# Scoring two neighbouring chunks back to back, so that the tensor array changes shape less often

## Chip, cores, metric

One core of a Trainium2 chip. The metric is the device time of one execution in microseconds (us), as the median of the runs; the profile's span (first to last instruction) is some 1.75 us shorter than the time of the same run.

## The reference

A retention layer followed by a mixer, for 4 batches of 768 positions, 8 heads of 64:

```python
state = gamma * state + k_t v_t^T          # per head, t = 0..767
y_t   = q_t @ state / sqrt(64)
u  = x + (x^T @ U @ V)^T                   # x: y of all heads, 768 x 512; rank 32
out = u + relu(u @ w_ch1) @ w_ch2          # 512 -> 2048 -> 512
```

The kernel computes the retention in six chunks of 128 positions a batch: a chunk's scores (k against q, masked causally), times v, plus q times the state that the chunks before have left.

## The kernel before

The attention of batch b runs inside the MLP of batch b-1. The MLP is a list of pieces with costs; each attention step is tied to a fraction of the total cost and goes out at the first piece boundary past it. The parts that matter, cut ("..."):

```python
RINGS = {"mlp": [0, 1, 2], "s": [3, 4], "o": [5], "qk": [6], "st": [7],
         "A": [6, 0], "B": [1], "C": [2]}      # PSUM banks by use; "mlp": [6, 0, 1, 2] for batches 2, 3
def score(b, ci):
    kT, qT = live["k", b, ci // 2][:, ci % 2], q_cols(b, ci)
    sp = [bank("s") for _ in range(2)]
    for h in range(H):                         # 8 matmuls on 64 rows of the array
        r = ds(D * (h % 2), D)
        nc.tensor.matmul(sp[h % 2][:, ts(h // 2, P)], kT[r, h // 2], qT[r, h // 2], ...)
    for i in range(2):                         # 2 masks on VectorE, 128x512 each
        a = rmid.tile([P, 4, P], bf16, tag=f"a{i}", bufs=2, ...)
        nc.vector.tensor_tensor(a, four(sp[i]), causal(mask), op=ALU.mult)
def mix(b, ci):                                # 4 matmuls of q with the state (not for chunk 0),
    o_p = bank("o")                            # 8 of the masked scores with v
    ...
    evac("A", xs[b][:, ci], o_p)               # ScalarE copies the bank out
...
# MLP 1 and 2: 32 "up" pieces (relu on ScalarE, each 4th on VectorE), sums of gT on VectorE
# after pieces 12-15, 16-19, 24-27, two after 31 and one after each of the first two of the 21
# products on the banks A, B and C that follow:
def p1(i): product("A", i, a11, w11, True);  keep("A", i, "a", i, 0)   # keep: VectorE reads A
def p2(i): product("B", i, a12, w21, True);  give("B", i, i, 0, held["a", i])
def p6(i): product("A", i, s2, t2, False);   keep("A", i, "b", i, 1)   # adds to what p1 left in A
order = [(p1, 0), (p1, 1), (p2, 0), (p6, 0), (p6, 1), ...]
...
for f, d in ((state, lag[0]), (score, lag[1]), (mix, lag[2] + more)):
    tracks.append(([part(f, b, i)], at[i] + d, at[i] + d))             # chunk by chunk
```

## Time and profile before

| | before |
|---|---|
| time, runs of the first comparison | 222.66, 223.40, 223.43, 223.38 us |
| span of the profile | 220.9 us |
| PE from the first MLP-up matmul to the last matmul (starts) | 189.52 us |
| switches between array shapes in that stretch | 58, together 5.46 us |
| PE waits over 60 ns in it | 2.47 us in 10 places |

TensorE (PE) carries the kernel. A matmul of N columns normally takes N/2.4 + 2.5 ns to the next start (the medians of the profile of before are 29, 56, 109 and 216 ns for 64, 128, 256 and 512 columns). What lies above that is a switch, where the number of active rows or columns changes, or a wait. Short waits never show as idle time, since a matmul's tail covers some 0.16 us (a 512-column matmul is shown with 0.38 us and the next starts after 0.216).

### The profile page before, as it was taken

The page shows a single profiled execution, that of the slowest core. Times are in us where ns is not written, and L with a number is a line of the kernel's source. Part 1 is how long each engine was busy: PE and PEld are TensorE (multiplying, and loading weights), DVE is VectorE, ACT ScalarE, POOL GpSimd, SP SyncE. Part 2 cuts the span into 40 slices and gives each one's busy share as a digit, 9 for nine tenths or more (in the row PEclk, how much of TensorE's full clock was granted, in tenths as well). Part 3 has the DMA queues.
Part 4 walks back from the last instruction along what each step waited for, and adds up shares of the span by engine and source line. Part 5 has one row for each costly group of instructions (what it writes and reads, how often), then busy time and mean ns, then how long its engine had stood idle before and what let it go on. Part 6 is the DMA issues. An engine that isn't in the chain of part 4 may idle for free.

```text
span 220.9 us, 5520 instructions
## 1 busy us (share of the span) xinstructions
PE 213.1 (96%) x2235; PEld 147.5 (67%) x2235; DVE 146.6 (66%) x306; ACT 91.1 (41%) x187; POOL 83.0 (38%) x121
## 2 busy tenths in 40 slices
PE   6879999999999999999999999999999999999994
PEld 2568754596555554656778884756788856668884
DVE  7578666235775469698896856498868542867443
ACT  3347654475655314775712005767420035551000
POOL 5457869796978767000099900000000000000000
PEclk9999999999999999999999999999999999999999
DMA  6999899999999989999999587900001951000043
GB/s 169 301 293 298 279 356 246 326 380 223 230 235 239 244 195 236 178 324 254 214 238 202 140 186 188 129 0 3 1 3 48 155 205 23 4 0 0 11 158 119
DMA packets 84489, 38.82 MB, mean 176 GB/s; under 512 B 58384, under 2 KB 77552, under 8 KB 84464
## 3 DMA queue, kind: packets, MB, share of 16 engines
q1 hardware_dynamic: 83456, 36.84, 70.7%
q10 hardware_dynamic: 1008, 1.64, 2.2%
q8 instruction: 17, 0.28, 0.6%
q14 instruction: 8, 0.07, 0.1%
HBM read 27.46 MB, written 6.29 MB: 153 GB/s over the span
## 4 chain that ended last, share of the span: by engine, by line
PE 85%; DVE 8%; DMA 2%; ACT 2%; issue 1%; SPq 1%; DVEq 0%; ACTq 0%
PE mlp L755 35%; PE A L647 13%; PE mlp L803 8%; PE C L647 6%; PE B L647 3%; DVE a L512 3%; DMA in<-in_q_dram 2%; PE s L506 2%; DVE gS L600 2%; PE o L528 2%; ACT qT L85 2%; PE st L490 1%; PE mlp L193 1%; PE qk L465 1%; PE o L523 1%
## 5 line engine op out<-in xcount | busy, mean ns | idle before, releaser
L755 PE MATMUL mlp<-uT,w1b 128*128 128x512 f16 (+1 forms) x512 | 88.7, 326 | 0.2 <-DVE gT L760 0.2
L762 ACT ACTIVATE gT<-mlp 128x512 f16<-128x512 f32 (+1 forms) x94 | 45.3, 490 | 59.3 <-PE mlp L755 57.1
L755 PEld LDWEIGHTS <-w1b 128*128 128x128 f16 x512 | 48.3, 98 | 31.1 <-issue 0.3
L760 DVE TENSOR_SCALAR gT<-mlp 128x512 f16<-128x512 f32 (+1 forms) x34 | 18.9, 555 | 27.1 <-PE mlp L755 26.7
L647 PEld LDWEIGHTS <-gT 128*128 128x128 f16 x288 | 27.6, 98 | 3.5
L512 DVE TENSOR_TENSOR a<-s,mask 128x512 bf16<-128x512 f32 x36 | 23.1, 682 | 7.8 <-PE s L506 7.7
L803 PE MATMUL mlp<-w2b,gT 128*128 128x512 f16 x96 | 24.4, 380 | 0.0
L85 ACT ACTIVATE x<-o 128x512 f16<-128x512 f32 x20 | 11.9, 596 | 23.6 <-PE o L528 23.5
L306 POOL TENSOR_TENSOR kd<-in,gk 128x512 bf16<-128x512 f32 x18 | 19.2, 1074 | 5.1 <-DMA in<-in_k_dram 4.2
L647 PEld LDWEIGHTS <-gS 128*128 128x128 f16 x200 | 19.2, 98 | 2.6
L306 POOL TENSOR_TENSOR qd<-in,gq 128x512 bf16<-128x512 f32 x18 | 19.5, 1099 | 1.3 <-DMA in<-in_q_dram 1.2
L647 PE MATMUL A<-w2t,gT 128*128 128x256 f16 x144 | 18.2, 273 | 0.0
L85 ACT ACTIVATE state<-st 64x256 bf16<-64x256 f32 x40 | 15.0, 375 | 5.4 <-PE st L386 3.2
L803 PEld LDWEIGHTS <-gT 128*128 128x128 f16 x96 | 8.1, 98 | 6.9
L304 POOL CAST vd<-in 128x512 bf16<-128x512 f32 x18 | 11.5, 649 | 1.1 <-DMA in<-in_v_dram 0.9
L346 POOL CAST w2b<-in 128x512 f16<-128x512 f32 x16 | 9.6, 613 | 2.0 <-DMA in<-in_moe_w_ch_dram 1.3
L340 POOL CAST w1b<-in 128x512 f16<-128x512 f32 x16 | 9.4, 613 | 2.3 <-DMA in<-in_moe_w_ch_dram 1.9
L647 PE MATMUL B<-w2b,gT 128*128 128x256 f16 x72 | 9.3, 273 | 0.0
L647 PE MATMUL A<-w2t,gS 128*128 128x256 f16 x72 | 9.2, 273 | 0.0
L647 PE MATMUL A<-w2b,gT 128*128 128x256 f16 x72 | 9.0, 273 | 0.0
L565 DVE TENSOR_TENSOR x<-s,x 128x256 f16<-128x256 f32 (+1 forms) x16 | 8.1, 548 | 1.2 <-issue 0.7
L600 POOL COPY gate<-gT 128x1 f16<-128x1 f16 x1 | 0.2, 190 | 22.5 <-DVE gT L760 22.5
(147 smaller groups left out, 283.4 us busy)
## 6 DMA issues: line engine op xcount, KB each, us to landing
in<-in_moe_w_ch_dram SPq DMA_DIRECT2D x32, 256.0 KB, 5.6
in<-in_k_dram SPq DMA_DIRECT2D x24, 256.0 KB, 5.4
in<-in_q_dram SPq DMA_DIRECT2D x24, 256.0 KB, 4.7
in<-in_v_dram SPq DMA_DIRECT2D x24, 256.0 KB, 5.4
out_dram<-o SPq DMA_DIRECT2D x16, 256.0 KB, 2.2
out_dram<-o ACTq DMA_DIRECT2D x6, 256.0 KB, 2.4
out_dram<-o SPq DMA_DIRECT2D x3, 128.0 KB, 1.7
Uf<-in_moe_U_dram SPq DMA_DIRECT2D x1, 96.0 KB, 5.5
```

The source lines that it names most:

```text
L85: nc.scalar.activation(dst, src, AF.Copy)
L304: nc.gpsimd.tensor_copy(out=t, in_=src)
L306: nc.gpsimd.tensor_tensor(t, src, g, op=ALU.mult)
L340: nc.gpsimd.tensor_copy(out=w1b[:, c, ts(mb, 512)], in_=take("w1", mb, c))
L346: nc.gpsimd.tensor_copy(out=w2b[:, m], in_=take("w2", m))
L512: nc.vector.tensor_tensor(a, four(sp[i]), causal(mask), op=ALU.mult)
L565: nc.vector.tensor_tensor(us[b][:, ds(j0, nj), ts(c, P)], four(grown[b][c])[:, :nj], xs[b][:, ds(j0, nj), ts(c, P)], op=ALU.add)
L647: nc.tensor.matmul(acc[key, i], lhs[:, m, ts(i, P)], rhs[:, m], start=(fresh and m == 0), stop=(m == NH - 1), skip_group_check=True)
L755: nc.tensor.matmul(g_p[:, :sz], w1b[:, c, ts(m, P)], uTs[b][:, ds(j, nj), c], start=(c == 0), stop=(c == NCB - 1))
L760: nc.vector.tensor_relu(gT[:, m, ds(lo, sz)], g_p[:, :sz])
L762: nc.scalar.activation(gT[:, m, ds(lo, sz)], g_p[:, :sz], AF.Relu)
L803: nc.tensor.matmul(ch, gT[:, m, ts(j, P)], w2b[:, m], start=(m == 0), stop=(m == NM - 1))
```

## The change

Intent: a score matmul uses 64 of the array's 128 rows, and going to that shape and back costs PE time. Two chunks scored in one go pay it once. The second chunk's scores need two more banks, so they borrow one of the MLP's and the one of mix; these are masked first. All six chunks of batches 2 and 3 and the first four of batch 1 go in pairs. The steps get new fractions, and after a pair ScalarE takes three relus in a row ("spare").

```diff
-    def score(b, ci):
+    def score(b, ci, tags=("s", "s")):
-        sp = [bank("s") for _ in range(2)]
+        sp = [bank(t) for t in tags]
...
+    def score_two(b, ci):
+        score(b, ci + 1, ("mlp", "o"))
+        score(b, ci)
+        screen(b, ci + 1)        # the masks; tiles a0, a1 now with bufs=3
+        screen(b, ci)
+        spare[0] = 3 if b > 1 else 0
...
+                if spare[0]:
+                    spare[0] -= 1
+                    n[0] -= n[0] % (3, 4, 4, 4)[b] == 0
-                if n[0] % (3, 4, 4, 4)[b] == 0:
+                if n[0] % (3, 4, 4, 4)[b] == 0 and not spare[0]:
                     nc.vector.tensor_relu(gT[:, m, ds(lo, sz)], g_p[:, :sz])
...
+                two = [(0.255, 0.39, 0.52), (0.1, 0.27, 0.44)][b - 2]
...
+                if b > 1:
+                    p = two[i // 2]
+                    steps = [(state, p + (-0.035, 0.02)[i % 2]),
+                             (mix, p + (0.083, 0.108)[i % 2])]
+                    if i % 2 == 0:
+                        steps.append((score_two, p))
+                elif i < 4:
+                    p = at[i | 1] + lag[1]
+                    steps = [(state, at[i] + lag[0]),
+                             (mix, p + (0.055, 0.07)[i % 2])]
+                    if i % 2 == 0:
+                        steps.append((score_two, p))
+                else:                                # chunks 4, 5 of batch 1 as before
...
-            t = at[-1] + lag[2]                      # low-rank part follows the last mix
+            t = at[-1] + lag[2] if b == 1 else two[-1] + 0.108
```

More of the change, by code (lines that the diff above doesn't have):

```diff
@@ L507, in score, with screen @@
                              qT[r, h // 2], start=True, stop=True)
+        live["sp", b, ci] = sp
+    def screen(b, ci):
+        sp = live.pop(("sp", b, ci))
         live["a", b, ci] = []
         for i in range(2):
-            a = rmid.tile([P, 4, P], bf16, tag=f"a{i}", bufs=2,
+            a = rmid.tile([P, 4, P], bf16, tag=f"a{i}", bufs=3,
                           name=f"a{i}_{b}_{ci}")
@@ L513, in score, with score_one @@
             live["a", b, ci].append(a)
+    spare = [0]
+    def score_one(b, ci):
+        score(b, ci)
+        screen(b, ci)
+    def score_two(b, ci):
+        score(b, ci + 1, ("mlp", "o"))
+        score(b, ci)
+        screen(b, ci + 1)
+        screen(b, ci)
+        spare[0] = 3 if b > 1 else 0
     def mix(b, ci):
@@ L980 @@
                 for sc in range(NSC):
-                    d = at[2 * sc] - 0.05 if sc else at[0]
+                    d = two[sc] - (0.04, 0.05, 0.05)[sc]
                     tracks.append(([lambda b=b, sc=sc: q_order(
@@ L984 @@
             for i in range(NCK):
-                more = 0.012 if b == 1 and i in (0, 2) or b == 2 else 0.0
-                if b == 2 and i == 4:
-                    more = 0.022
-                for f, d in ((state, lag[0]), (score, lag[1]),
-                             (mix, lag[2] + more)):
-                    tracks.append(([part(f, b, i)], at[i] + d, at[i] + d))
-            t = at[-1] + lag[2]
+                more = 0.012 if b == 1 and i in (0, 2) else 0.0
+                if b > 1:
[11 more added lines that the diff above has]
+                else:
+                    steps = [(state, at[i] + lag[0]),
+                             (score_one, at[i] + lag[1]),
+                             (mix, at[i] + lag[2] + more)]
+                for f, d in steps:
+                    tracks.append(([part(f, b, i)], d, d))
+            t = at[-1] + lag[2] if b == 1 else two[-1] + 0.108
             if b == 1:
```

## The prediction

> **What bounds the kernel now.** I read the page's busy shares first, then the TensorE (PE) timeline, then the chain of work that ended last, then the VectorE (DVE) timeline where that chain leaves PE. From the page, engine shares and the chain by engine:
>
> ```profile
> PE 213.1 (96%) x2235; PEld 147.5 (67%) x2235; DVE 146.6 (66%) x306; ACT 91.1 (41%) x187; POOL 83.0 (38%) x121
> ...
> PEclk9999999999999999999999999999999999999999
> ...
> PE 85%; DVE 8%; DMA 2%; ACT 2%; issue 1%; SPq 1%; DVEq 0%; ACTq 0%
> ```
>
> PE is the bound, at full clock. A busy share of 96% does not mean that no PE time can be saved: matmuls overlap, so a gap shorter than a matmul's tail never appears as idle. It shows in the distance between starts. PE timeline, batch 2 (columns: start us, length us, engine, line):
>
> ```profile
> 96.09 0.39 PE L490 MATMUL st<-vd,kd 128*128 128x128 bf16 x4
> 96.31 1.89 PE L755 MATMUL mlp<-uT,w1b 128*128 128x512 f16 x8
> 98.04 0.40 PE L528 MATMUL o<-vd,a 128*128 128x64 bf16 x8
> 98.37 0.40 PE L506 MATMUL s<-qO,kT 64*128 64x128 bf16 x8
> 98.70 1.04 PE L755 MATMUL mlp<-uT,w1b 128*128 128x512 f16 x4
> ```
>
> Four state matmuls on the full array take 96.31-96.09 = 0.22 us, 55 ns each. The eight score matmuls (64 rows; in the trace two of them start 3 ns apart, then 52 to 63 ns pass) take 98.70-98.37 = 0.33 us, not 4 x 0.055 = 0.22. Taking all starts in the trace, the last score matmul is followed 148 ns later by a full-array one, 93 ns more than 55; and the matmul before a score group occupies 96 ns more than its own kind does elsewhere (512 columns: 312 instead of 217 ns). So each switch into 64-row tiles and back costs 0.096 + 0.093 = 0.19 us of PE time. With 18 chunks in batches 1 to 3 that is 3.4 us. This is what the change is after.
>
> The other PE gaps, above the switch cost, in the parts the change touches (start-to-start excess in the trace): batch 1 within MLP 0: 0.29 and 0.36 us (a key transpose waits until ACT has emptied the bank of the query transpose), 0.16 and 0.28 us (mix waits for the masked scores); batch 2: 0.33 us (an MLP bank waits for DVE's relu) and 0.09 + 0.54 us (the last scores wait for an "s" bank); batch 3: none. Sum 2.05 us. The 0.64 us one, in the chain of batch 2:
>
> ```profile
> 109.50 0.44 DVE gT L760
> ...
> 110.03 0.57 DVE gS L600
> 110.62 1.28 DVE gS L600
> 111.90 0.35 DVE da L660
> ...
> 112.28 0.94 DVE gT L600
> 113.22 1.21 DVE a L512 x2
> ...
> 114.47 0.38 PE s L506 x7
> ```
>
> Here DVE's queue (two of the sums at L600, a keep at L660, another sum, two masks at L512) decides when PE goes on. One sum takes 1.28 us instead of 0.56, as GpSimd starts the next batch's preparation at 110.17.
>
> **What the Trainium skill says.** "TensorEngine Tiling (Array Packing)", Key Properties: changing the tiling mode drains TensorE. The trace agrees: 0.19 us in and out, and nothing between matmuls of one mode. "TensorE: Matmul & The Clock Gate", Part 1: warm starts are N/2.4 + about 2.5 ns apart, 56 ns for 128 columns and 216 for 512; the trace has 55 and 217. "PSUM — Partial Sum Buffer", Engine vs sequencer instructions: ScalarE and VectorE queues are strict FIFO and matmuls run in program order; the trace above agrees, since a mask behind sums holds PE. "SBUF — State Buffer", SBUF: two separate sides: a VectorE op with two SBUF inputs and a GpSimd op exclude each other; the 0.56 to 1.28 us at 110.62 agrees.
>
> **The change part by part.** I placed every step by its fraction of the MLP's cost between the MLP's pieces (the same arithmetic gives the old order as the timeline shows it).
>
> (1) Switches. Batches 2 and 3 go from 6 score groups to 3 each, the first four chunks of batch 1 from 4 to 2: 8 entries and exits less, 8 x 0.19 = **-1.51 us**, all on PE. No matmul is added or taken away: two scores back to back take 0.55 us plus the entry.
>
> (2) Batch 1. Four masks now follow one score group: the first starts 0.43 us after the scores begin (52.25 to 52.68 in the trace), the pitch is 0.60, so the third ends at 2.31 and the fourth at 2.91 us if DVE is free. The pair's own chunk is masked last, and its mix comes first.
> - The two key transposes that waited for ACT now have a double score (+0.22 us) ahead of them: 0.29 and 0.36 become about 0.08 and 0.14.
> - Mixes 0 and 1 (fractions 0.670 and 0.685 of 41.47) both fall on the piece boundary 28.51, with no piece between. They share the single "o" bank; from a mix's start to the end of ACT's copy is 0.43 + 0.60 us (54.32 to 55.35), and mix 0's matmuls take only 0.23. Mix 1 waits about **0.86 us**; new.
> - For the second pair a weight sum and the 0.69 us residual add stand before the masks, as before at 67.12 to 68.06, so the fourth mask ends 3.5 us after the scores begin. Two pieces, a transpose and two groups of four bring PE to it at about 3.2: 0.38 us. The old 0.16 and 0.28 go.
> Stalls in batch 1: 1.08 before, 1.46 after.
>
> (3) Batch 2. The DVE relu that held a bank for 0.33 us goes to ACT for three pieces (597 ns on ACT against PE's 866 a piece, so ACT keeps up). Mix 1 follows mix 0 by one half piece and four state matmuls, 0.66 us, plus 0.23 of mix, against 1.09: 0.2 us. Query copies just before the second pair: 0.1. The third pair is the costly one: it sits right after the last MLP-up piece and so behind the two sums (0.56 + 1.28). Masks start 2.4 us after the scores begin. The borrowed MLP bank is the one that product p2 needs; PE is there at 0.55 + 2 x 0.87 = 2.29 and the first mask ends at 3.1: 0.87 us. Then p6 adds to the bank that p1's keep must read first, and that keep is behind all four masks: 2.4 + 4 x 0.60 + 0.41 = 5.2 against p2's end at 4.0: 1.26 us. Before, only 0.64 was lost there. Stalls: 0.96 before, 2.4 after.
>
> (4) Batch 3. GpSimd has finished, all pairs lie within MLP-up and the mixes are 3.4 to 4 us behind; I find 0.06 us. Before none.
>
> The earlier place of the low-rank part (some 4 us in batch 3) hides nothing that PE waits for: the transitions at 131.7 and 178.5 us have no gap but the switch.
>
> Sum: -1.51 - 2.05 + 3.92 = +0.36 us at face value. The new stalls are differences of two queue positions that I add up, and a stall lets DVE and ACT catch up before the next; I take a fifth off the new ones (3.1 us). Net -1.51 - 2.05 + 3.1 = about **-0.4 us**. From a base of 223.2 (between the mean 223.16 and the median 223.4): **222.8 us**.
>
> **Rivals.**
> - The switches are saved and the longer distance to the mixes takes all DVE waits away: -1.51 - 2.05 = -3.6, so 219.6 us. For it: DVE is 66% busy, ACT 41%, and the borrowed banks take the "s" wait away. Against: the order of mixes 0 and 1 in batch 1 and p6 behind four masks in batch 2 follow from program order and strict queues. I think 221.5 to 222 more likely than this extreme.
> - DVE becomes the bound where four masks (2.48 us in a burst) meet the sums at L600: other relus late, MLP banks late, 2 us more stalls than I count in batches 2 and 3: 225.2. For it: the chain in batch 2 is on DVE already. Against: spare hands three relus to ACT after each pair.
> - Switches turn out hidden (the array drains while weights load): saving nothing, 224.3. Against: the 93 and 96 ns are start-to-start on PE, in program order.
>
> **Range and chances.** PE runs in program order, so the time moves by saved switches less the change in stalls. The saving is sure to a tenth; the stalls to about 1.5 us either way, which gives 221.3 to 224.4 with the 0.8 us spread of the runs of before. Two per cent is 4.5 us: more than switches and all removed stalls together (3.6), so faster by 2% is nearly excluded, and slower by 2% needs new stalls of 8 us.
>
> **What would show it.** Right on (1): in the changed PE timeline 10 groups of score matmuls in place of 18 in batches 1 to 3 (8 of 16 matmuls, of about 0.55 us to the next start). Right on (2): about 0.9 us of PE waiting for ACT's x copy between the first two mixes of batch 1. Right on (3): PE waiting for DVE's masks and the keep at L660's successor after the last up piece of batch 2, some 2 us, with no "s" bank wait. Right on (4): no gap over 0.1 us in batch 3. It would be wrong if keep and mix waits were absent (time near 220.5), or if gaps appeared at MLP-up banks in batches 2 and 3.

## The result, and the profile after

| | before | after |
|---|---|---|
| time, median of runs | 223.39 us | 223.69 us (223.50 to 223.75) |
| ratio, 95% interval | | 1.002 (0.9998 to 1.0041) |
| span of the profile | 220.9 us | 222.0 us |
| first MLP-up to last matmul | 189.52 us | 190.69 us |
| switches in it | 58, 5.46 us | 42, 3.95 us |
| waits over 60 ns in it | 2.47 us | 5.39 us |

Ratios are the mean time of one kernel's runs over that of the other's in the same rounds, so not quite the ratio of the medians quoted. Executions over 1.5% slower than the fastest of the same kernel are left out of the means. The change neither gained nor clearly lost. It did save its switches: 16 fewer of them, 1.51 us. It paid with 2.92 us of waits; a further 0.24 us, what is left of the difference, came off in distances under 60 ns. Some 0.11 of it lies inside the pairs: one takes 0.553 us from its first score to the next full-array matmul, two single groups take 2 x 0.330, which is 0.107 more, and only 0.093 of that is the switch; this leaves 0.014 us for each of eight pairs. -1.51 + 2.92 - 0.24 = +1.17 us, the difference of the two stretches.

From the page of the changed kernel, busy shares and the chain by engine:

```profile
PE 211.7 (95%) x2235; PEld 147.8 (67%) x2235; DVE 145.2 (65%) x305; ACT 91.2 (41%) x188; POOL 83.2 (37%) x121
...
PE 47%; DVE 1%; issue 0%
```

PE's busy time fell and so did its share: the time lost is waiting. The chain adds up to 48% only; followed back, it ends half-way through the span, so here it can't be compared with the 85% of before, and the timelines have to do. The waits one by one, read from the starts in the trace (us; 0 stands for less than 0.06; the last column is the same kernel profiled again later; two that both kernels share, 0.23 us at mix 5 of batch 1 and 0.08 to 0.13 at a product, are left out):

| wait of PE | before | predicted | after | again |
|---|---|---|---|---|
| batch 1: query transpose (chunks 2, 3), for GpSimd's q | 0.11 | not seen | 0.755 | 0.842 |
| key transpose behind it, for ACT | 0.29 | 0.08 | 0.075 | 0.073 |
| mix 1, for ACT's copy of mix 0 | 0 | 0.86 | 0.849 | 0.849 |
| key transpose of chunks 4, 5, for ACT | 0.36 | 0.14 | 0.139 | 0.141 |
| mixes 2 and 3, for their masks | 0.16 + 0.28 | 0.38 | 0.378 | 0.373 |
| batch 2: mix 1, for ACT's copy | 0 | 0.2 | 0.187 | 0.188 |
| second pair, for the query copy | 0 | 0.1 | 0.217 | 0.210 |
| MLP bank behind a relu; "s" bank | 0.33; 0.64 | 0; 0 | 0; 0 | 0; 0 |
| third pair, for bank "o" | 0 | not seen | 0.108 | 0.107 |
| product p2, for the borrowed bank | 0 | 0.87 | 0.705 | 0.704 |
| product p6, for the keep behind four masks | 0 | 1.26 | 1.255 | 1.254 |
| batch 3: mixes | 0 | 0.06 | 0 | 0 |
| first MLP-up of the MLP after batch 2 | 0 | not seen | 0.364 | 0 |

The column "before" is one profile. In the two others with its order in batch 1 (before_again and split_scores below) the waits of mixes 2 and 3 were 0.70 and 0.87 us and not 0.44. A weight sum on VectorE ahead of these masks took 0.41 us in the profile of before and 0.75 in before_again.

The costliest spot, PE after the third pair of batch 2, changed kernel:

```profile
110.70 1.92 PE L664 MATMUL A<-w2b,gT 128*128 128x256 f16 x16
113.16 1.03 PE L664 MATMUL B<-w2b,gT 128*128 128x256 f16 x8 [0.54 <-DVE a L516]
115.28 1.03 PE L664 MATMUL A<-w2t,gS 128*128 128x256 f16 x8 [1.09 <-DVE da L677]
```

and VectorE in the same stretch:

```profile
110.63 0.56 DVE L617 TENSOR_TENSOR gS<-gT 128x768 f16<-128x768 f16 x1
111.22 1.28 DVE L617 TENSOR_TENSOR gS<-gS,gT 128x768 f16<-128x768 f16 x1
112.43 0.68 DVE L516 TENSOR_TENSOR a<-mlp,mask 128x512 bf16<-128x512 f32 x1
113.03 0.68 DVE L516 TENSOR_TENSOR a<-o,mask 128x512 bf16<-128x512 f32 x1
113.63 1.27 DVE L516 TENSOR_TENSOR a<-s,mask 128x512 bf16<-128x512 f32 x2
114.82 0.41 DVE L677 TENSOR_TENSOR da<-A,x 128x256 f32<-128x256 f32 x1
```

Read across: p2 starts at 113.16, just after the first mask (112.43 + 0.68 = 113.11) frees the borrowed bank. p6 starts at 115.28, just after the keep (114.82 + 0.41 = 115.23), which stood behind two sums and four masks. The same spot before is shown in the prediction, from 109.50 us on. The idle time in brackets is shorter than the wait in the table, as the tail of the matmul before covers part of it.

Batch 1, PE, changed kernel: the query transposes, then mix 0 and mix 1.

```profile
56.85 0.27 PE L465 MATMUL qk<-ident,qd 128*128 128x128 bf16 x2
57.72 0.51 PE L465 MATMUL qk<-ident,qd 128*128 128x128 bf16 x6 [0.59 <-POOL qd L306]
...
61.83 0.40 PE L545 MATMUL o<-vd,a 128*128 128x64 bf16 x8
62.91 0.38 PE L540 MATMUL o<-state,qO 128*128 128x128 bf16 x4 [0.69 <-ACT x L85]
```

The same place before:

```profile
52.25 0.40 PE L506 MATMUL s<-qO,kT 64*128 64x128 bf16 x8
...
54.32 0.40 PE L528 MATMUL o<-vd,a 128*128 128x64 bf16 x8
...
57.59 0.73 PE L465 MATMUL qk<-ident,qd 128*128 128x128 bf16 x8
```

Mix 1 waits for ACT as foreseen. The wait at 57.72 was not. GpSimd prepared q at the same time in both kernels (before, then after; the two halves end at 55.34 + 2.41 = 57.75 and 55.44 + 2.22 = 57.66):

```profile
55.34 2.41 POOL L306 TENSOR_TENSOR qd<-in,gq 128x512 bf16<-128x512 f32 x2
```

```profile
55.44 2.22 POOL L306 TENSOR_TENSOR qd<-in,gq 128x512 bf16<-128x512 f32 x2
```

What differs is when PE arrives: 57.59 before, 56.85 after. Before, the scores and the mix of chunk 0 came ahead of these transposes (52.25 and 54.32); now they come behind them. They are 0.43 us with their switch and 0.23 us of work, which had filled the time until q arrived.

### The profile page after: what moved, and what is told of

It is laid out like the page before. It is cut to its first block, busy times and chain, and to the rows that moved or that the text cites. A ratio compares the mean times of both kernels' runs of the same rounds, so it can differ in the third digit from the quotient of the medians.

```text
span 222.0 us, 5519 instructions
## 1 busy us (share of the span) xinstructions
PE 211.7 (95%) x2235; PEld 147.8 (67%) x2235; DVE 145.2 (65%) x305; ACT 91.2 (41%) x188; POOL 83.2 (37%) x121
## 5 line engine op out<-in xcount | busy, mean ns | idle before, releaser
L782 ACT ACTIVATE gT<-mlp 128x512 f16<-128x512 f32 (+1 forms) x95 | 45.8, 492 | 67.0 <-PE mlp L772 48.8
L780 DVE TENSOR_SCALAR gT<-mlp 128x256 f16<-128x256 f32 (+1 forms) x33 | 18.2, 553 | 28.7 <-PE mlp L772 28.2
L516 DVE TENSOR_TENSOR a<-s,mask 128x512 bf16<-128x512 f32 x20 | 12.8, 682 | 1.7 <-PE s L506 1.7
L828 DVE TENSOR_TENSOR o<-mlp,x 128x512 f32<-128x512 f32 x6 | 4.1, 690 | 7.1 <-PE mlp L823 7.1
```

Source lines behind the costliest of these rows:

```text
L780: nc.vector.tensor_relu(gT[:, m, ds(lo, sz)], g_p[:, :sz])
L782: nc.scalar.activation(gT[:, m, ds(lo, sz)], g_p[:, :sz], AF.Relu)
```

## The experiments

Two rivals to "the waits in the table are what the saved switches were paid with" were in play: that switches cost nothing, so there was nothing to gain, and that the new waits are run-to-run variation. Times of kernels of one job are beside the same runs of the kernel before: its median was 223.19 us in the first job (before_again to split_scores), 222.96 in the second (pool_later to no_spare), 223.54 in the third (the last three, on another chip). All ratios are to these runs. The changed kernel ran only in the first comparison (ratio 1.002) and in the third job (1.0038), so elsewhere it is safer to compare ratios, or waits in the traces, than medians.

**before_again** (no edit).

> The kernel before once more, against itself. Of the 1.12 us between the two profiled spans, 0.64 us lies in one wait of batch 1: the first query transpose after the first key chunks waits for GpSimd's preparation of q (0.755 us in the changed kernel, 0.111 us in the profile of before), though the change leaves the order of GpSimd's work up to there as it was. Theory A, arrival of the inputs varies from run to run: this profile shows that wait at any value between 0.1 and 0.8 us, and the times spread over some 0.7 us (the four of before: 222.66 and three of 223.38 to 223.43). Theory B, the change causes it: the wait is 0.1 us again here. Ratio 1.000 either way.

Measured: 223.57 us, ratio 1.0028 (1.0006 to 1.005) against itself, so differences of 0.3% are not to be trusted here, even where the interval leaves out 1. The wait for q was below 60 ns in this profile (PE at 57.54, q ready at 57.00), 0.111 us in the first and 0.455 us in split_scores below, which has the order of before (PE at 57.53, q ready at 58.04). So in these three profiles q's arrival varies by a microsecond, and PE's hardly at all.

**mix_apart**: the first mix of batch 1 one piece earlier.

```diff
-                             (mix, p + (0.055, 0.07)[i % 2])]
+                             (mix, p + (0.05, 0.07)[i % 2])]
```

> The changed kernel with the first mix of batch 1 one piece earlier, so that a piece of the MLP lies between mixes 0 and 1. Theory (the single bank of the mixes, emptied by ACT, holds PE for 0.849 us): that wait goes, a wait of mix 0 for its masks of 0.1 to 0.2 us comes, so 0.65 us faster than the changed kernel: about 223.0. Rival (the waits before mix 1 are made up elsewhere, since the next transposes wait for ACT anyway): no change, 223.7.

Measured: 223.38 us, ratio 1.0014 (0.9989 to 1.0038), no clear difference from the changed kernel. The wait of mix 1 fell from 0.849 to 0.497 us, not to nothing, and mix 0 did not wait for its masks. ScalarE and PE of this kernel:

```profile
62.30 0.78 ACT L85 ACTIVATE state<-st 64x256 bf16<-64x256 f32 x2 [0.49 <-PE st L490]
...
63.10 0.60 ACT L85 ACTIVATE x<-o 128x512 f16<-128x512 f32 x1
...
63.75 0.38 PE L540 MATMUL o<-state,qO 128*128 128x128 bf16 x4 [0.33 <-ACT x L85]
```

One piece earlier, mix 0 comes right after the state's matmuls, and ACT's copies of the state stand ahead of the copy that mix 1 needs. The trace confirms the mechanism (one bank, emptied by ACT); the gain at this wait is 0.35 us, not 0.65. In this profile q came late, at 58.79, and its wait of 0.28 + 0.88 us hid the gain in the span (222.7).

**third_single**: chunks 4 and 5 of batch 2 one at a time, at the old fractions, with the low-rank part back there too.

```diff
+                    if b == 2 and sc == 2:
+                        d = at[4] - 0.05
...
+                if b == 2 and i > 3:
+                    steps = [(state, at[i]), (score_one, at[i] + 0.04),
+                             (mix, at[i] + 0.1 + (0.022, 0.012)[i % 2])]
-                if b > 1:
+                elif b > 1:
...
-            t = at[-1] + lag[2] if b == 1 else two[-1] + 0.108
+            t = at[-1] + lag[2] if b < 3 else two[-1] + 0.108
```

> The changed kernel with chunks 4 and 5 of batch 2 scored one at a time, at the places of before. Theory (the third pair sits behind the last sums and in front of the first keeps in the VectorE queue, costing 0.705 + 1.255 + 0.108 us against 0.64 of before): 2.07 - 0.64 = 1.43 us less waiting, 0.19 more of switches, so 1.2 us faster than the changed kernel: about 222.5, and 222.1 if the 0.36 us at the start of the next MLP goes with it, as the low-rank part returns to its old place too. Rival (the sums and keeps, not the pair, set the pace there): less than 0.3 us.

Measured: 222.19 us as the median of all six runs, 221.97 of the five fast ones; ratio 0.9966 (0.9938 to 0.9993). The slow run (225.42) is left out of the ratio. The waits of p2 and p6 are gone. A single score waits 0.344 us for its bank, and a new wait of 0.823 us stands at the first product:

```profile
110.05 1.03 PE L664 MATMUL A<-w2b,gT 128*128 128x256 f16 x8 [0.66 <-ACT gT L782]
```

ACT's copies for mix 3 and for the state now stand between the last relus. By the ratios (0.9966 beside 1.002) the gain over the changed kernel is 1.2 us, by the medians of two sets of runs 1.7; 1.2 to 1.6 was expected. But it came with waits that I had not listed, and with no wait for q in its profile.

**split_scores**: the kernel before, with each score group of batch 3 cut in two.

```diff
...
+                if b == 3:
+                    hs = range(H // 2, H)
+                    d = at[i] + lag[1] - 0.022
+                    tracks.append(([part(score, b, i, range(H // 2))], d, d))
...
```

> The kernel before with each score group of batch 3 cut into two groups of four matmuls, the first one to two MLP pieces earlier. Six switches to 64-row tiles and back are added, nothing else. Theory (0.096 + 0.093 us of PE for each): +1.13 us over before, 224.5 beside 223.4. Rival (switches are hidden): no change. In the PE starts: 18 + 6 groups, each with 96 ns before and 93 ns after it.

Measured: 224.73 us, ratio 1.0075 (1.0059 to 1.0091), or 1.7 us above before where 1.13 was expected; the rest is not the switches': its profile also waits 0.34 us more for q and 0.43 more for the masks in batch 1, which the edit does not touch. Twelve more changes of shape (58 to 70) took 6.60 instead of 5.46 us: 1.14 us, 0.19 for each in and out. PE of this kernel:

```profile
136.48 0.28 PE L508 MATMUL s<-qO,kT 64*128 64x128 bf16 x4
136.69 1.04 PE L759 MATMUL mlp<-uT,w1b 128*128 128x512 f16 x4
137.66 0.28 PE L508 MATMUL s<-qO,kT 64*128 64x128 bf16 x4
137.88 2.76 PE L759 MATMUL mlp<-uT,w1b 128*128 128x512 f16 x12
```

Four score matmuls hold PE for 0.22 us, two thirds of the 0.33 that eight do, and the piece between takes 0.97 instead of 0.87. The rival that switches are hidden falls.

**pool_later**: GpSimd is let go after the last sum, not after the last relu.

```diff
-            if b == 1:
-                late(pieces, len(pieces) - 1, [part(
-                    nc.gpsimd.tensor_copy, out=gate, in_=gT[:, NM - 1, S - 1:])])
...
             late(down, 0, [s3, s4])
+            if b == 1:
+                late(down, 1, [part(nc.gpsimd.tensor_copy, out=gate,
+                                    in_=gS[:, 2, NH - 1, :1])])
```

> The changed kernel with GpSimd's preparation of batch 3 let go only after the last sum of batch 2's MLP (its gate reads that sum), some 5 us later. Theory (GpSimd lengthens the sum ahead of the masks from 0.56 to 1.28 us, the wait of p6 for the keep behind four masks is there without it): the wait of product p2 for its bank falls from 0.705 us to 0.15 or less, that of p6 stays between 1.1 and 1.4 us, the time falls 0.6 us, to 223.1. Rival (GpSimd has no part in it): both waits stay. Risk: the key and query transposes of batch 3 come later and may hold PE at its start.

Measured: 222.89 us, ratio 0.9992 (0.9959 to 1.0024). VectorE and PE of this kernel (times of PE: p2, then p6):

```profile
111.41 0.56 DVE L617 TENSOR_TENSOR gS<-gS,gT 128x768 f16<-128x768 f16 x1
...
114.28 0.41 DVE L677 TENSOR_TENSOR da<-A,x 128x256 f32<-128x256 f32 x1
```

```profile
112.64 1.04 PE L664 MATMUL B<-w2b,gT 128*128 128x256 f16 x8
114.75 1.03 PE L664 MATMUL A<-w2t,gS 128*128 128x256 f16 x8 [1.07 <-DVE da L677]
```

The sum takes 0.56 us, p2 no longer waits, and p6 waits 1.235 us as before: GpSimd made p2's wait. That the four masks ahead of the keep made p6's follows from VectorE's order, and from third_single, where no pair stands there and the wait is gone.

**batch3_single**: batch 3 as before.

```diff
+                if b == 3:
+                    steps = [(state, at[i]), (score_one, at[i] + 0.04),
+                             (mix, at[i] + 0.1)]
-                if b > 1:
+                elif b > 1:
...
-        spare[0] = 3 if b > 1 else 0
+        spare[0] = 3 if b == 2 and ci < 4 else 0
```

(the query copies and the low-rank part of batch 3 go back as well)

> The changed kernel with batch 3 as before: six single score groups. In batch 3 the change brought no wait over 0.1 us and took none away, so here the saved switches stand alone. Theory: three switches more, 3 x 0.19 = 0.57 us slower than the changed kernel: 224.25. Rival (switches hidden, or the pairs' longer distance to the mixes hides other things): no change.

Measured: 224.54 us, ratio 1.0067 (1.0021 to 1.0114). Six more changes of shape took 4.52 instead of 3.95 us, 0.57, and batch 3 has no wait over 60 ns. So the pairs of batch 3 are a plain gain. The times differ by somewhat more: 0.85 us between the medians, 1.05 by the ratios (1.0067 beside 1.002), from two sets of runs.

**turns_as_before**: only the low-rank part of batch 2 back at its old fraction.

```diff
-            t = at[-1] + lag[2] if b == 1 else two[-1] + 0.108
+            t = at[-1] + lag[2] if b < 3 else two[-1] + 0.108
```

> The changed kernel with the low-rank part of batch 2 (projection, growth, adds, transposes) back at its old fraction, 1.8 us later. The changed kernel waits 0.364 us before the first MLP-up matmul of batch 2's MLP; the second transpose of uT was issued 125.94 us and its data landed 133.6 us, 0.1 us before that matmul's weights. Theory C (the earlier place puts the transposes among the output stores[...]): the wait goes, 0.36 us faster, 223.35. Theory D (the landing varies from run to run): the wait comes and goes, no clear difference. Theory E (it is VectorE's last give, which the profile names): the wait stays.

Measured: 223.46 us, ratio 1.0011 (0.9973 to 1.0048), no clear difference; the wait is gone in its profile. But it is also absent in no_spare and in after_again, which have the early place. Over all profiles the wait was 0.36, 0.25, 0.08, 0.39, 0.11, 0 and 0 us at the early place, and 0 in all six at the old one. The transposes of uT, in the view of that tensor from 120 to 136 us, before and then after:

```profile
DMA to landing us min/median/max: 3.2/4.3/5.3
```

```profile
DMA to landing us min/median/max: 3.2/5.6/7.6
```

The releaser that the profile of the changed kernel names (VectorE's last give, L685) can't be the cause: before, the same matmul starts at 131.95 us, while that give runs from 131.83 to 132.25. That early transposes meet the output stores would fit the longer landing (7.6 beside 5.3 us at most), but seven against six profiles of a wait that varies don't settle it.

**no_spare**: no relus handed to ACT.

```diff
-        spare[0] = 3 if b > 1 else 0
+        spare[0] = 0
```

> The changed kernel without handing relus to ACT after a pair. In batch 2 each pair falls after 16, 24 and 32 MLP-up pieces, where the next three are ACT's anyway, so the hand-over does nothing there; in batch 3 it only moves the relus of VectorE. Theory: the same time within 0.2 us, 223.7. Rival (VectorE would hold MLP banks without it): new waits for relus in batch 3, 0.5 us or more slower.

Measured: 223.98 us, ratio 1.0055 (1.0013 to 1.0097). My expectation fell: batch 3 has a new wait of 0.435 us. VectorE, then PE:

```profile
158.32 0.68 DVE L780 TENSOR_SCALAR gT<-mlp 128x512 f16<-128x512 f32 x1
...
159.06 0.60 PE L772 MATMUL mlp<-uT,w1b 128*128 128x256 f16 x4 [0.27 <-DVE gT L780]
```

A relu left to VectorE stood behind four masks and a sum, and an MLP piece needed its bank. The waits of batch 2 are the same to 0.01 us without the hand-over, so there it does nothing, as the count of pieces said.

**after_again** (the changed kernel, no edit).

> The changed kernel once more. If its waits follow from its order, the profile shows again 0.85 us at mix 1 of batch 1, 0.7 and 1.25 us after the third pair of batch 2; the two that hang on transfers move: the first query transpose anywhere from 0 to 1 us, the first MLP-up of the next batch from 0 to 0.4 us. Time 223.7, give or take 0.4.

Measured: 223.71 us, ratio 1.0038 (0.9999 to 1.0078). The waits that follow from the order came back to 0.01 us (last column of the table above); the one of the next MLP did not.

**first_single**: chunks 0 and 1 of batch 1 one at a time.

```diff
-                elif i < 4:
+                elif 1 < i < 4:
```

> The changed kernel with chunks 0 and 1 of batch 1 scored and mixed one at a time, at the places of before. The wait of the first query transpose ends when GpSimd has prepared q: 57.75 us before, 57.66 after. What differs is when PE gets there: the scores (0.33 + 0.10 us) and the mix (0.23 us) of chunk 0 came ahead of it before and come behind it now, 0.66 us. Theory F (work that filled the wait was moved behind it): the wait is 0.65 us shorter than in the changed kernel's profiles (0.1 to 0.3 us, where those show 0.55 to 1.16 us in six of seven), the wait at mix 1 goes (0.85), the key transpose's wait comes back (0.29 instead of 0.08), a switch comes back (0.19): together 1.1 us faster than the changed kernel, 222.6. Rival (the arrival alone, theory A): 0.45 us faster, as only mix 1's wait goes, and the transpose still waits some 0.7 us.

Measured: 222.78 us, ratio 0.9977 (0.9948 to 1.0006), 0.93 us below the changed kernel of the same job. PE of this kernel:

```profile
58.62 0.61 PE L465 MATMUL qk<-ident,qd 128*128 128x128 bf16 x8
```

The eight query transposes go without a wait (q was ready at 56.78), mix 1's wait is gone, the key transpose waits 0.287 us. PE reached the transposes at 58.62 because its first MLP-up matmul came 1.1 us later here than in the changed kernel (29.34 against 28.24), so this profile alone doesn't prove the 0.65 us. Nor do the times: 0.93 us lies between the 1.1 of theory F and the 0.45 of its rival. All profiles together do: where chunk 0 is scored ahead, PE came at 57.53 to 58.62 in five profiles and waited 0.11, 0, 0.455, 0 and 0; where it is scored behind, PE came at 56.85 to 57.56 in eight, and waited 0.755, 0.842, 1.16, 0, 0.679, 1.0, 0.878 and 0.546, the 0 being a run in which q was ready at 56.35. Mended2 below is the fifth of the first set. Counted from the first MLP-up matmul, PE came after 29.28 us in all five of the first set and after 28.61 to 28.62 in all eight of the second: 0.67 us earlier, the work that was moved. When q is ready varies by itself (56.78 to 58.04 us in the first set, 56.35 to 58.79 in the second, there 0.4 later on average), so not all of the difference between the waits of the two sets is the order's.

**mended2**: pairs only where the runs so far led me to expect no extra wait: chunks 0, 1 of batch 1 and 4, 5 of batch 2 single, and two mixes of batch 2 moved.

```diff
 (third_single and first_single, and)
-                             (mix, p + (0.083, 0.108)[i % 2])]
+                             (mix, p + (0.083, 0.108)[i % 2]
+                              + (b == 2 and i < 4) * (0, 0.007, 0, 0.041)[i % 4])]
```

> What the runs point to as best: pairs where they cost no wait (chunks 2 and 3 of batch 1, 0 to 3 of batch 2, all of batch 3), single scores for chunks 0 and 1 of batch 1 and 4 and 5 of batch 2; mix 3 of batch 2 behind the first product as before (in third_single ACT's copy for it and the states delayed the last relu, and the product waited 0.82 us), mix 1 of batch 2 half a piece later. Against before: six switches less (-1.2 us), waits in batch 1 0.75 instead of 1.03 us (0.29 key transpose, 0.14, 0.38, less the old 0.16, 0.36, 0.28 gone; 0.24 stays), in batch 2 0.64 + 0.2 instead of 0.97. Sum -1.6 us: 221.6 beside 223.2, ratio 0.993. Rival (pairs bring waits wherever they are put): within 0.5 us of before.

Measured: 221.69 us, ratio 0.9936 (0.9909 to 0.9963) against before, where 0.993 was expected. That is below 2%, but its interval lies clear of 1 and of the changed kernel's (1.0038, 0.9999 to 1.0078, in the same job). 46 changes of shape (4.33 us) and 2.14 us of waits: it keeps 1.13 us of the 1.51 and waits no more than before. The size came as expected, the places not quite: the 0.64 us expected at the "s" bank is not there, and 0.629 us stands at the first product instead (for ACT's relu, behind the state's copies). The other large one is 0.395 us at the second pair of batch 2, 0.18 more than in the changed kernel. The profile names ACT's relu for it, but the borrowed bank is one of a ring of four and its own relu had ended 1.84 us before. It is the query copy, as in the changed kernel: in all ten profiles with this pair the scores start 0.146 or 0.147 us after VectorE's copy of q ends (here 102.197 and 102.343), while ACT's named relu ends only 0.01 to 0.02 us before them, where every other wait checked shows 0.05 or more from releaser to start. With mix 1 moved half a piece later, its wait (0.187 us in the changed kernel) is gone, so PE comes to this pair that much earlier and waits 0.18 us longer for a copy that VectorE's queue makes no sooner; the move gained nothing.

## Why the prediction was right or wrong

- **The time** lay in the range (221.3 to 224.4) but 0.9 us above the central 222.8: a small gain was forecast, and none came. The sum at face value, 223.2 + 0.36 = 223.6, was within 0.1 us, which is partly luck: it lacks 1.0 us of waits that the profile after shows (0.64 and 0.36, below), and the profiles differ by more than the timed medians do.
- **Switches, right.** Predicted -1.51 us, measured 5.46 - 3.95 = 1.51, and both tests by count (split_scores +1.14, batch3_single +0.57) give the same 0.19 us each. The rival of hidden switches is out.
- **Batch 1, right as far as it went.** All four waits after came within about 0.01 us. What they rest on is program order, strict queues and durations from the trace of before. The working shown is a little looser than that: 1.03 - 0.23 is 0.80 and not 0.86, and the 0.87 and 1.26 of batch 2 are likewise some 0.06 us above the differences shown. The term left out fits the 0.05 us from a releaser's end to PE's start in the lines above (113.11 to 113.16, 115.23 to 115.28). The 0.38 was rough too (3.5 - 3.2 is 0.3), so its hit is in part luck. And the waits that the change removed were read from one profile, where those of mixes 2 and 3 were the smallest of three.
- **Batch 1, the step missed.** The part by part account moved chunk 0's score and mix to later places and asked only what they then wait for, not what they had been covering. The 0.11 us in front of the query transposes is not even in its list of waits; without the 0.66 us of work ahead of them it became 0.755. This is the largest wait that the prediction missed, +0.64 us.
- **Batch 2, right in mechanism and nearly in size**: p6 1.26 against 1.255, p2 0.87 against 0.705; the query copy's wait was 0.1 too small and the 0.108 us for bank "o" was not foreseen. These last belong together in part: PE, held up for bank "o", comes to p2 that much later and waits that much less there. pool_later shows which part is GpSimd's. One reason was wrong: the 0.33 us relu wait did not go because of the hand-over to ACT, which does nothing in batch 2; it went with the new places of the steps.
- **Batch 3, right**: no wait. The hand-over, which part (4) doesn't name though the second rival does, is what keeps it so (no_spare, 0.435 us).
- **"Hides nothing that PE waits for", wrong in part.** The earlier low-rank part came with up to 0.39 us of waiting in five of seven profiles; whether it causes them is not settled.
- **The discount of a fifth, wrong.** I took 0.8 us off the new waits since a wait lets the other queues catch up. In the places that the account covered, the waits after sum to 3.91 us (the 0.108 included), against 3.92 worked out: the small misses cancel (p2 and batch 3 too long, the query copy and bank "o" too short), and no catching up is seen. The ledger closes: -1.51 - 2.05 + 3.91 + 0.64 (q) + 0.36 (next MLP), with 0.05 more at one later product and 0.24 off in small distances, is 1.16, against the +1.17 of the profiles. The timed medians differ by less (0.30 and 0.17 us in the two comparisons); the profile of before was one of the fastest runs of its kernel (222.64).
- **The rival of -3.6 us** (waits all vanish) is out; **DVE as the bound** took place in one spot, after the third pair of batch 2, which part (3) had counted; the 2 us of further waits that the rival adds did not come (its 225.2 is also not that sum, 222.8 + 2 being 224.8).

## What to carry to other kernels

When steps on the bounding engine are regrouped, list for each moved step what it waits for at its new place and also what wait it was filling at its old one; the second list is the one that gets forgotten. Work out queue waits from program order and durations; here the sum as it stood fitted the waits that it covered better than the discounted one. A batching that saves a fixed cost is worth it only where the burst behind it (here four masks) does not stand in front of an instruction that the bounding engine needs soon, so pair in some places and not in others.

## What the Trainium skill lacked or had wrong

- "TensorEngine Tiling (Array Packing)", Key Properties, says that changing the mode drains TensorE, but gives no cost. Here it is 0.096 us on entering and 0.093 on leaving 64-row tiles with 128-column matmuls (1.14 us for six groups added, 1.51 us for eight taken away).
- "SBUF — State Buffer", SBUF: two separate sides, is right on VectorE and GpSimd; the runs add the size for one case: a 128x768 16-bit sum took 1.28 us with GpSimd preparing and 0.56 without, and that alone was 0.70 us of PE time.
- None has it, and it is a figure of this program's order more than of the chip: how long a burst on a strict-FIFO engine holds PE. Four masks of 0.60 us pitch ahead of one 0.41 us keep cost PE 1.254 to 1.256 us in seven profiles with GpSimd running beside it and 1.235 in the one without.
